# Attention and a long convolution on one core: a range guard with a second path, and three rewrites around the normalisation

## The chip, the cores and the metric

The kernel runs on one core of a Trainium2 chip. A core has five engines that run side by side, each with its own queue of instructions: PE (TensorE, the matrix unit; PEld in the profile is its weight load), DVE (VectorE), ACT (ScalarE), POOL (GpSimd) and SP (SyncE, which here only issues DMAs). They wait for one another through semaphores. The metric is device time of one execution in microseconds (us); less is better.

## The reference

Two independent results stand side by side in the output, columns 0 to 511 and 512 to 1023:

```python
# A: attention, S = 2048 tokens, D = 512, H = 32 heads of 16
qkv = (x @ wqkv) ...                                   # q, k, v of every head
scores = einsum("bhqd,bhkd->bhqk", q, k) * (Dh ** -0.5)
p = softmax(scores, axis=-1)
a = einsum("bhqk,bhkd->bhqd", p, v) ... @ wo
# B: a short and a long causal convolution with gates
kv = k_shift * v            # k_shift: 4 taps
y = long causal convolution of kv with ssm_k (per channel, length S) + kv * ssm_D
b = q * y
```

The inputs x and the weights have a standard deviation of 0.05, so q and k have 0.05 * 0.05 * sqrt(512) = 0.057, and a score is some thousandths. Every exponential is close to 1, and each row sum is close to 2048 times the constant factor with which the kernel scales its exponentials.

## The kernel before

**Attention.** The 32 heads are taken in 32 groups `n`; a group is four heads (one for each 32-row strip of the matrix unit) times 512 queries. Scores are made transposed, keys on partitions: one block is 128 keys by 512 queries of one head, so that a group has 16 x 4 = 64 blocks and the whole problem 2048. Four blocks of different heads can run beside each other on the four row strips (`qk_mm`, L838). A block's exponential is taken in one of two ways:

- on ACT, `exp` of two or three blocks (128x1024 or 128x1536) in one instruction from the PSUM banks into `PT` (`emit_exp`, L865);
- on DVE, one block per step at most: L901 reads the bank and makes a 16-bit fixed-point number in `PTD`, and for two blocks at a time three passes over SBUF (L929 mantissa, L934 square, L938 octave) make of it two float16 factors' terms, so that such a block goes into the next product as two matmuls of half weight.

The product with V (PV, `emit_pv`, L977) accumulates in bank `PVB`: four heads on four column strips run beside each other when four matmuls of four different heads stand next to each other. I call such a set of neighbours a pass. V has columns of ones behind its 16, so the row sum of the exponentials (the softmax's denominator) comes out of the same accumulation.

When a group is complete, `finish_group` does the following on DVE: transpose the bank to `DT` (L1084), reciprocal of the sums into `DR` (L1091), product with the reciprocals into `DTN` (L1095), and, after each second group, a transpose of `DTN` back to `OTN` (L1104), which is the weight operand of the output projection (L521 as unit "op", L1161 at the end). The last group is finished in four parts of 128 queries (`finish_last`, L1118, L1125, L1128, L1133).

**Convolution.** It is 512 channels of Toeplitz products (L1252) from rows `WR` that SP fetches from a scratch in memory, 512 KB at a time; results go through L1267 (DVE), L1279 (PE) and L1286 (DVE).

**Who decides the order.** No engine schedules itself: the program is written out once by a planner in the same file, step by step. Step `T` is one exponential of ACT; between two steps the planner puts PV passes, projections, convolution lags and, where PE would idle, filler matmuls of zero weights (L1502) that keep the matrix unit's clock up. It keeps a clock of its own for each engine, from constants at the head of the file (how many blocks to look ahead `LOOK`, how many blocks of a group must be left so that DVE may take one `GAP`, how close to the next exponential PE may still be given work `MARGIN`, and so on). `flow` holds the DVE work that can be moved; `urgent` work is put in when it is due; `locking` notes a time in which POOL is busy, and passes of kind "p" (L929, L934, L938) are not started in it. `feed_wr` and `on_op` pace the 512 KB loads against the fetching of PE's instructions.

**The end.** After the last exponential come the last PV passes, the last part of `finish_last`, the last projection, two copies (ACT L1584, DVE L1582), two output DMAs, and SP's wait for all output DMAs.

## Time and profile before

| | us |
|---|---|
| median of 3 runs (738.21 to 739.79) | 738.93 |
| the profiled execution | 737.82 |
| its span, first to last instruction | 736.0 |
| busy: ACT / DVE / PE / POOL | 722.2 / 705.1 / 698.3 / 98.9 |
| ACT's exponentials: 483 of 128x1024, 200 of 128x1536, 3 of 128x2048 | 719.9 busy, 3.0 idle before them |
| granted clock of the matrix unit | 0.998 of full speed |

How to read it: the profile's busy time of a group of instructions counts overlaps once, while "mean ns" is the length of one, with the part that overlaps its neighbours. "Idle before" is the time in which the engine had nothing in flight ahead of an instruction of the group, and the name behind the arrow is what ended that wait. The rows themselves stand in the prediction.

### The profile page before, as it was taken

To read this page: it belongs to the slowest core of one execution; us is meant where nothing else is said; L and a number is where in the kernel's file an instruction comes from. 1 tells how busy PE (TensorE), PEld (TensorE's weight loads), DVE (VectorE), ACT (ScalarE), POOL (GpSimd) and SP (SyncE) were. 2 spreads that over 40 slices of the span, in tenths; PEclk is the share of its full clock that TensorE was granted. 3 is DMA by queue.
4 is the path that set the end of the run, shared out by engine and by line. 5 is a ranking of instruction groups with operands and counts; after the bars stand their busy time and mean duration, and the time that the engine had idled before them with its cause. 6 is when DMAs were issued, how large, how long until landed. Compare 5 with 4: busy or idle time off the path is not lost.

```text
span 736.0 us, 32656 instructions
## 1 busy us (share of the span) xinstructions
PE 698.3 (95%) x14748; PEld 317.9 (43%) x14755; DVE 705.1 (96%) x1449; ACT 722.2 (98%) x690; POOL 98.9 (13%) x172
## 2 busy tenths in 40 slices
PE   8999999999999999999999999999999999999997
PEld 4333344445444444444444344444433443434455
DVE  3999999999999999999999999999999999989996
ACT  6999999999999999999999999999999999999997
POOL 7202102010023002001201300220021202010000
PEclk9999999999999999999999999999999999999999
DMA  9899655678797788677676777775857775585211
GB/s 181 227 253 307 173 194 189 218 235 251 264 258 263 245 285 244 229 229 260 181 225 217 228 261 231 229 264 167 294 188 261 238 263 179 201 273 193 103 45 32
DMA packets 73721, 161.50 MB, mean 219 GB/s; under 512 B 34064, under 2 KB 37776, under 8 KB 73200
## 3 DMA queue, kind: packets, MB, share of 16 engines
q1 hardware_dynamic: 66400, 150.43, 63.7%
q0 software_dynamic: 5984, 8.66, 4.0%
q8 instruction: 117, 1.92, 1.0%
q10 hardware_dynamic: 1200, 0.33, 0.2%
q14 instruction: 20, 0.16, 0.1%
HBM read 142.61 MB, written 6.42 MB: 202 GB/s over the span
## 4 chain that ended last, share of the span: by engine, by line
ACT 64%; DVE 24%; PE 10%; issue 0%
ACT PT L865 64%; DVE PTD L901 10%; DVE PTD L934 5%; PE PS L838 3%; DVE PTD L938 3%; DVE PTD L929 3%; PE PS L977 3%; PE PS L1252 2%; DVE KV L609 1%; DVE DT L1084 1%; PE PS L521 1%; PE PS L682 1%; DVE KTo L596 0%; DVE VA L625 0%; PE PS L1502 0%
## 5 line engine op out<-in xcount | busy, mean ns | idle before, releaser
L865 ACT ACTIVATE PT<-PS 128x1024 bf16<-128x1024 f32 (+2 forms) x686 | 719.9, 1261 | 3.0 <-PE PS L838 2.0
L901 DVE TENSOR_SCALAR PTD<-PS 128x512 uint16<-128x512 f32 x470 | 313.7, 680 | 7.8 <-PE PS L838 7.5
L838 PE MATMUL PS<-QT,KTo 32*128 32x512 bf16 (+2 forms) x2248 | 270.0, 365 | 20.3 <-ACT PT L865 9.5
L977 PE MATMUL PS<-PT,VA 128*32 128x512 bf16 (+2 forms) x1733 | 185.6, 369 | 1.9 <-DVE VA L625 1.3
L1252 PE MATMUL PS<-WR,KV 128*26 128x128 bf16 (+8 forms) x8192 | 186.7, 219 | 0.7 <-issue 0.5
L1252 PEld LDWEIGHTS PS<-WR,KV 128*32 128x32 bf16 (+7 forms) x8192 | 136.3, 94 | 56.6 <-issue 32.7
L934 DVE TENSOR_TENSOR PTD<-PTD 128x1024 f16<-128x1024 f16 x235 | 157.5, 678 | 0.1
L977 PE MATMUL PS<-PTD,VA 128*32 128x512 f16 (+1 forms) x1030 | 152.8, 363 | 0.5 <-DVE PTD L938 0.5
L838 PEld LDWEIGHTS PS<-QT,KTo 32*128 32x128 bf16 x2248 | 71.4, 91 | 180.5 <-ACT PT L865 121.6
L374 POOL DMA_DIRECT2D QT<-QS x120 | 61.0, 516 | 356.3 <-DVE QS L587 354.5
L938 DVE TENSOR_SCALAR PTD<-PTD 128x1024 uint16<-128x1024 uint16 x235 | 95.6, 411 | 0.2
L929 DVE TENSOR_SCALAR PTD<-PTD 128x1024 uint16<-128x1024 uint16 x235 | 93.5, 415 | 0.1
L977 PEld LDWEIGHTS PS<-PT,VA 128*32 128x32 bf16 x1733 | 46.6, 94 | 91.6 <-issue 74.2
L1502 PE MATMUL PS<-IDN,ZW 128*32 128x128 bf16 (+3 forms) x223 | 48.4, 298 | 0.0
L977 PEld LDWEIGHTS PS<-PTD,VA 128*32 128x32 bf16 x1030 | 40.9, 95 | 9.4 <-DVE PTD L938 1.4
L374 POOL DMA_DIRECT2D out_dram<-OUTA x15 | 8.9, 591 | 113.9 <-DVE OUTA L1169 113.9
L1502 PEld LDWEIGHTS PS<-IDN,ZW 128*32 128x32 bf16 x223 | 17.0, 96 | 14.8 <-issue 7.9
L1084 DVE STREAM_TRANSPOSE DT<-PS 128x512 f32<-128x512 f32 x31 | 21.9, 706 | 0.3 <-PE PS L977 0.2
L521 PE MATMUL PS<-xT,WKV 128*32 128x512 bf16 (+1 forms) x256 | 18.4, 376 | 3.7 <-DVE DT L1084 2.2
L575 PE MATMUL PS<-WKV,xT 128*128 128x128 bf16 x256 | 19.3, 220 | 1.5 <-DVE DT L1084 0.6
L521 PE MATMUL PS<-xT,WQ 128*32 128x512 bf16 x240 | 17.9, 384 | 2.4 <-DVE DT L1084 2.0
L575 PEld LDWEIGHTS PS<-WKV,xT 128*128 128x128 bf16 x256 | 14.4, 98 | 9.0 <-issue 3.8
(72 smaller groups left out, 243.1 us busy)
## 6 DMA issues: line engine op xcount, KB each, us to landing
WR<-kz_scratch SPq DMA_DIRECT2D x256, 512.0 KB, 5.3
KV<-KV SPq DMA_DIRECT2D x16, 256.0 KB, 6.6
kz_scratch<-WR SPq DMA_DIRECT2D x1, 2176.0 KB, 8.3
QN<-in_B_q_dram POOLq DMA_DIRECT2D x8, 256.0 KB, 5.2
out_dram<-QN POOLq DMA_DIRECT2D x8, 256.0 KB, 3.1
QT<-QS POOLq DMA_DIRECT2D x120, 16.0 KB, 4.3
out_dram<-OUTA POOLq DMA_DIRECT2D x15, 128.0 KB, 3.0
QN<-in_B_ssm_k_dram SPq DMA_DIRECT2D x1, 1024.0 KB, 7.7
```

What stands on the lines that cost most here:

```text
L374: f(outp, inp).then_inc(dsem.sem, 16)
L521: ins = e.matmul(dst[g:g + 32], lhsT=w[:, g:g + 32], rhs=rhs, tile_position=(0, g), **kw)
L575: ins = e.matmul(PS[:, bank, 128 * j:128 * j + 128], lhsT=xT[:, dc, (4 * sc + j) * 128:(4 * sc + j + 1) * 128], rhs=WV[:, dc, o * 128:(o + ...
L838: ins = e.matmul(PS[:, bank, i * w:i * w + w], lhsT=KTo[32 * s:32 * s + 32, OF[n_] % 2, kt * 128:(kt + 1) * 128], rhs=QT[32 * s:32 * s + 3 ...
L865: h = act.op(lambda e: e.activation(PT[:, p0:p0 + n, :], src, ACT.Exp, scale=EXP_SCALE, bias=EXP_BIAS), [h, free], us=(0.065 + 0.4257 * n, ...
L901: h_f = urgent(lambda e: e.tensor_scalar(fix_u, PS[:, bank, :], FIX_ADD, FIX_HI, ALU.add, ALU.min), [h, h_ptd.get(i - R_PTD)], slack=S_FX)
L929: st["h"] = dve.op(lambda e: e.tensor_scalar(mant_u, fix_u, MANT, HALF_BITS, ALU.bitwise_and, ALU.bitwise_or), [st["h"]], us=us)
L934: st["h"] = dve.op(lambda e: e.tensor_tensor(mant, fix, mant, ALU.mult), [st["h"]], us=us)
L938: h = dve.op(lambda e: e.tensor_scalar(fix_u, fix_u, OCTAVE, ONE_MORE, ALU.bitwise_and, ALU.bitwise_or), [st["h"]], us=us)
L977: ins = e.matmul(dst, lhsT=w, rhs=rhs, start=first, stop=last, tile_position=(0, 32 * s))
L1252: ins = e.matmul(PS[32 * g:32 * g + 2 * ((30 - d) // 2 + 1), BGB, 128 * kk:128 * kk + w], lhsT=kv, rhs=WR[:, (4 * qd + g) % R_W, S - 64 * ...
L1502: pe.op(lambda e, s=s, k=k, rhs=rhs, bank=bank, rows=rows, c0=c0, first=first: e.matmul(PS[32 * s:32 * s + rows, bank, c0:c0 + 128 * k], l ...
```

## The change

**The guard.** The kernel's two exponentials hold only while the row sums stay in a range. The changed kernel checks each reciprocal: `all_ok` puts four small instructions on POOL after every second group (and for each part of the last): clamp the reciprocals to the range, subtract, compare with zero, add to a count `OKS`. Behind everything else DVE sums the count (L1643), subtracts it from what it must be (L1644), PE adds that over the partitions (L1646), DVE turns it into an integer `BADI` (L1648), and each of the five engines loads that word into a register and branches: on zero to the end, otherwise into a second program that does the attention again with the exact maximum of each row. Ahead of the branch (2 planned operations on POOL and SP, 3 on ACT, 24 on DVE, 40 on PE) stands a prefetch hint for the branch. SP's wait for the output DMAs comes after the branch. With the given inputs the row sums are near 2048 * 2^-2 * 1.507 = 772, and the accepted range is 32 to 16384.

**Pair transposes.** q's columns are written in another order (`halves`, `in_pairs`), so that two heads' 16-bit values stand next to each other and the transpose back to `OTN` can move 32-bit pairs: 128x256 instead of 128x512 elements.

**Products with the reciprocals on POOL.** In `finish_group` L1095 moves from DVE to POOL (L1142), under `locking`; `DR` gets four buffers instead of two. In the last group they stay on DVE.

**PV gathered.** In `pv_step` a pass with fewer than four members is held back unless the ring of `PTD` buffers is full or the group must close; groups that must close wait up to three more steps for their DVE blocks.

Some planner constants change too.

```diff
-LOOK = 30
+DV_FREE = 0
+CLOSE_ALL = 1
+LOOK = 28
+HARD = 3
+LATE_BY = 0.2
-GAP = 20
+GAP = 18
-MARGIN = 0.15
+MARGIN = 0.1
-SLACK = 1.5
+SLACK = 2.0
+HOLD = 1.0
+HELD = 2
+MULT = (0.8, 0.95)
...
+    def halves(x):
+        return x.rearrange("p (a h i) -> p a h i", h=2, i=32)
+    def in_pairs(x):
+        return x.rearrange("p (a i h) -> p a h i", i=32, h=2)
...
-                if len(run) < 4 and not close and not old and len([x for x in bl if x[0] in on_dve]) < DV_MIN and T < end[0]:
+                if len(run) < 4 and not close and not old and T < end[0] and (len([x for x in bl if x[0] in on_dve]) < DV_MIN or ring_free() > DV_FREE):
+                    break
+                if CLOSE_ALL and len(run) < 4 and close and not late and not old and len(bl) < len([x for x in acts + dves if sub(x[0]) == (n, j)]) and n < NL:
                     break
...
+    def all_ok(n, r, h):
+        w = r.shape[1]
+        a, b, c = (OKS[:, i, 0:w] for i in range(3))
+        h_ok[n] = pool.op(lambda e: e.tensor_scalar(a, r, 1.0 / D_MOST, 1.0 / D_LEAST, ALU.max, ALU.min), [h, h_okn[0]], us=(0.1, 0.2))
+        h_ok[n] = pool.op(lambda e: e.tensor_tensor(b, a, r, ALU.subtract), [h_ok[n]], us=(0.1, 0.2))
+        h_ok[n] = pool.op(lambda e: e.tensor_scalar(a, b, 0.0, None, ALU.is_equal), [h_ok[n]], us=(0.1, 0.2))
+        h_ok[n - 1] = h_ok[n] = h_okn[0] = pool.op(lambda e: e.tensor_tensor(c, c, a, ALU.add), [h_ok[n], h_okn[0]], us=(0.1, 0.2))
...
         def mult(us):
             r = n % 2
-            h_mul[n] = dve.op(lambda e: e.tensor_tensor(
...
+            h_mul[n] = locking(pool.op(lambda e: e.tensor_tensor(
+                heads_of(dtn, r), halves(dt)[:, :, :, 0:DH], over(DR[:, n % 4, :], 8), ALU.mult), [st["h"], h_otn.get(p - 2)], us=MULT), MULT[0] - 0.2)
...
-            h_otn[(p, i1)] = h_otn[p] = dve.op(lambda e: e.transpose(out=OTN[:, p, sl], in_=dtn[:, sl]), deps, us=us)
+            h_otn[(p, i1)] = h_otn[p] = dve.op(lambda e: e.transpose(out=OTN[:, p, sl].bitcast(PAIR), in_=dtn[:, sl].bitcast(PAIR)), deps, us=us)
...
-    for ds in d_outA + d_outB + [d_outE]:
-        sp.op(lambda e, ds=ds: e.wait_ge(ds.sem, ds.n), inc=False)
+    h_bad = dve.op(lambda e: e.tensor_reduce(OKS[:, 0, 0:1], OKS[:, 2, :], mybir.AxisListType.X, ALU.add), [h_okn[0]])
+    h_bad = dve.op(lambda e: e.tensor_scalar(BAD[:, :], OKS[:, 0, 0:1], -1.0, float(NQB * NG * 16), ALU.mult, ALU.add), [h_bad])
+    h_bad = pe.op(lambda e: e.matmul(PS[0:1, bank, 0:1], lhsT=BAD[:, :], rhs=VA[:, 0, 0, DH:DH + 1], start=True, stop=True),
+                  [h_bad, bank_free[bank]], kind="F")
+    h_bad = dve.op(lambda e: e.tensor_copy(BADI[:, :], PS[0:1, bank, 0:1]), [h_bad])
...
+    def decide(e, eng, geng, ahead):
+        eng.run(e, ahead)
+        e.wait_ge(*h_bad)
+        r = e.alloc_register("bad")
+        e.reg_load(r, BADI[0:1, 0:1])
+        names = [f"{e.engine.name}_{x}" for x in ("again", "over")]
+        e.br_eq(r, 0, names[1], names[0]).branch_hint(eng.hint)
+        with nc.body(names[0], valid_engines=[e.engine]):
+            geng.run(e)
+            e.br(names[1])
+        nc.switch_bb(names[1])
```

What the planner makes of it is shown by the order of the two built programs, at three places.

First, DVE and POOL at the end of a group. In the rows, `DT` is the transposed bank, `DR` the reciprocals, `DTN` the product, `PTD` the fixed-point blocks. DVE before, at the end of an odd group:

```order
L1084 STREAM_TRANSPOSE DT<-PS 128x512
L938 TENSOR_SCALAR PTD<-PTD 128x2x512
L1091 RECIPROCAL DR<-DT 128x16
L938 TENSOR_SCALAR PTD<-PTD 128x2x512
L609 TENSOR_TENSOR KV<-PS,OUTA 128x4x16x4 x2
L1095 TENSOR_TENSOR DTN<-DT,DR 128x16x16
L929 TENSOR_SCALAR PTD<-PTD 128x2x512
L1104 STREAM_TRANSPOSE OTN<-DTN 128x512
```

DVE now, at the end of an odd group:

```order
L1130 STREAM_TRANSPOSE DT<-PS 128x512
L956 TENSOR_SCALAR PTD<-PTD 128x2x512
L1137 RECIPROCAL DR<-DT 128x16
L961 TENSOR_TENSOR PTD<-PTD 128x2x512
L928 TENSOR_SCALAR PTD<-PS 128x512
L1155 STREAM_TRANSPOSE OTN<-DTN 128x256
```

and POOL now, over the same kind of place (`OKS` is the guard's scratch and count; QT and QN are the DMAs that POOL issues):

```order
L389 DMA QT<-QS 16x512 x8
L1142 TENSOR_TENSOR DTN<-DT,DR 128x8x2x16
L1120 TENSOR_SCALAR OKS<-DR 128x32
L1121 TENSOR_TENSOR OKS<-OKS,DR 128x32
L1122 TENSOR_SCALAR OKS<-OKS 128x32
L1123 TENSOR_TENSOR OKS<-OKS 128x32
L389 DMA QN<-in_B_q_dram 128x4x256 x4
L1142 TENSOR_TENSOR DTN<-DT,DR 128x8x2x16 x2
```

The product has left DVE's queue for POOL's, where the four guard instructions follow it; the transpose back on DVE now waits for POOL and has half the elements.

Second, PE around the end of a group (`QT,KTo` are scores, `PT,VA` and `PTD,VA` PV, `WR,KV` the convolution). Before:

```order
L838 MATMUL PS<-QT,KTo 128x512 x3
L977 MATMUL PS<-PT,VA 32x512 x13
L977 MATMUL PS<-PTD,VA 32x512 x3
L838 MATMUL PS<-QT,KTo 128x512 x3
L977 MATMUL PS<-PT,VA 32x512 x2
L977 MATMUL PS<-PTD,VA 32x512 x2
L1252 MATMUL PS<-WR,KV 20x128 x4
```

Now:

```order
L865 MATMUL PS<-QT,KTo 128x512 x3
L1004 MATMUL PS<-PT,VA 32x512 x7
L1004 MATMUL PS<-PTD,VA 32x512
L1004 MATMUL PS<-PT,VA 32x512 x3
L1004 MATMUL PS<-PTD,VA 32x512
L865 MATMUL PS<-QT,KTo 128x512 x3
L1004 MATMUL PS<-PT,VA 32x512 x2
L1004 MATMUL PS<-PTD,VA 32x512 x2
L1309 MATMUL PS<-WR,KV 12x128 x4
```

PV still comes in bursts of twelve and sixteen between two sets of scores; members of `PT` and `PTD` are now mixed so that a pass is full.

Third, DVE at the very end. Before:

```order
L1125 RECIPROCAL DR<-DT 128x4
L1128 TENSOR_TENSOR DTN<-DT,DR 128x4x16
L1133 STREAM_TRANSPOSE OTN<-DTN 128x128
L1169 CAST OUTA<-PS 128x512
L1582 CAST QT<-PS 128x256
L1589 UNCONDITIONAL_BRANCH
```

Now:

```order
L1184 STREAM_TRANSPOSE OTN<-DTN 128x64
L1639 CAST QT<-PS 128x256
L1643 TENSOR_REDUCE OKS<-OKS 128x1
L1644 TENSOR_SCALAR BAD<-OKS 128x1
L1648 CAST BADI<-PS 1x1
L1769 TENSOR_LOAD BADI
L1771 COMPARE_AND_BRANCH
```

Behind the last copy stand three more instructions with one of PE between them, and the branch on the loaded word.

Counted over the whole main path, from the two orders:

| | before | now |
|---|---|---|
| ACT exponentials 128x1024 / 128x1536 / 128x2048 | 483 / 200 / 3 | 485 / 198 / 3 |
| blocks on DVE (L901, now L928) | 470 | 472 |
| products with reciprocals on DVE / on POOL | 35 / 0 | 4 / 31 |
| guard instructions on POOL | 0 | 80 and one memset |
| copies of the convolution L1267 (now L1324): 512 / 384 / 256 / 128 wide | 6 / 6 / 7 / 8 | 5 / 6 / 6 / 14 |
| PV matmuls of 512 columns, and the passes they make | 2431 in 671 | 2434 in 631 |
| steps of a two-block exponential with 11 or more PV matmuls of 512 columns | 28 | 36 |
| filler matmuls (L1502, now L1559) | 223 | 255 |

## The prediction

> **What bounds the kernel now.** I read the page's busy shares first, then the groups of ACT and DVE with shapes kept apart, then the waits of ACT, then the timeline at the places where ACT had waited, and last the end of the program.

> ```profile
> span 736.0 us, 32656 instructions
> PE 698.3 (95%) x14748; PEld 317.9 (43%) x14755; DVE 705.1 (96%) x1449; ACT 722.2 (98%) x690; POOL 98.9 (13%) x172
> ACT 64%; DVE 24%; PE 10%; issue 0%
> ```

> ACT is busy 98% of the span and carries most of the chain that ended last. DVE and PE stand at 96% and 95%, but PE is topped up by fillers and DVE by blocks that the planner hands over. POOL is nearly free.

> ```profile
> L865 ACT ACTIVATE PT<-PS 128x1024 bf16<-128x1024 f32 x483 | 472.8, 1132 | 2.1 <-PE PS L838 1.3
> L865 ACT ACTIVATE PT<-PS 128x1536 bf16<-128x1536 f32 x200 | 295.1, 1562 | 0.4 <-PE PS L838 0.3
> L865 ACT ACTIVATE PT<-PS 128x2048 bf16<-128x2048 f32 x3 | 5.7, 1889 | 0.5 <-PE PS L838 0.5
> ```

> Only 3.0 us of idle time stand before 686 exponentials, so the kernel is one stream of ACT work with a head and a tail. Its rate comes from an undisturbed stretch:

> ```profile
> 599.08 41.91 ACT L865 ACTIVATE PT<-PS 128x1536 bf16<-128x1536 f32 x40
> L865 ACT ACTIVATE PT<-PS 128x1024 bf16<-128x1024 f32 x28 | 27.0, 1166 | 0.0
> L865 ACT ACTIVATE PT<-PS 128x1536 bf16<-128x1536 f32 x12 | 17.5, 1566 | 0.0
> 8.04 12.31 ACT L865 ACTIVATE PT<-PS 128x2048 bf16<-128x2048 f32 x10 [0.50 <-PE PS L838]
> 713.97 16.51 ACT L865 ACTIVATE PT<-PS 128x1024 bf16<-128x1024 f32 x17
> ```

> A third block in an instruction costs 1562 - 1132 = 430 ns. The 40 instructions (28 of two blocks, 12 of three) took 41.91 us; less 12 x 0.43, and less the 0.2 us by which the last one outlasts its turn, that is 0.914 us for a step of two blocks. The whole stream at that rate is 686 x 0.914 + 200 x 0.43 + 3 x 0.76 (1889 - 1132) + 0.2 = 715.5 us. It ran from 8.04 to 713.97 + 16.51 = 730.48, which is 722.4 us. So 6.9 us were lost in it, 3.0 of them as visible idle time and the rest as starts a little late, hidden in the overlap. The change can gain by fewer blocks on ACT, by less of these 6.9 us, or in the tail.

> **Where ACT lost time.** The largest loss in the stream is this one:

> ```profile
> 72.76 0.75 DVE L929 TENSOR_SCALAR PTD<-PTD 128x1024 uint16<-128x1024 uint16 x2
> 73.43 0.68 DVE L934 TENSOR_TENSOR PTD<-PTD 128x1024 f16<-128x1024 f16 x1
> 74.03 2.00 DVE L901 TENSOR_SCALAR PTD<-PS 128x512 uint16<-128x512 f32 x3
> 74.77 0.53 PE L838 MATMUL PS<-QT,KTo 32*128 32x512 bf16 x3 [0.94 <-DVE PTD L901]
> 75.34 1.02 ACT L865 ACTIVATE PT<-PS 128x1024 bf16<-128x1024 f32 x1 [0.66 <-PE PS L838]
> 76.64 19.37 ACT L865 ACTIVATE PT<-PS 128x1536 bf16<-128x1536 f32 x18 [0.27 <-PE PS L838]
> ```

> DVE ran passes without a gap, so the L901 that frees a bank came late, PE waited 0.94 us for it, and ACT stood still for 0.66 + 0.27 = 0.93 us. The other kind is smaller and more frequent, a burst of PV between two sets of scores:

> ```profile
> 422.46 4.19 ACT L865 ACTIVATE PT<-PS 128x1024 bf16<-128x1024 f32 x4
> 423.29 1.04 PE L977 MATMUL PS<-PT,VA 128*32 128x512 bf16 x13
> 424.27 0.10 PEld L838 LDWEIGHTS PS<-QT,KTo 32*128 32x128 bf16 x3 [0.42 <-issue]
> ```

> Sixteen PV matmuls (13, and 3 from PTD) held PE from 423.29 to 424.27; the four exponentials took 4.19 us where 4 x 0.914 + 0.2 = 3.86 were due, a loss of 0.33 us.

> **The change, part by part.** The profiled execution took 737.82 us with its span of 736.0, 1.11 us under the median of 738.93; I make the sum as a difference and add it to the median.

> *Blocks on ACT.* The order shows two blocks moved to DVE: 200 to 198 instructions of three blocks, 483 to 485 of two. With 686 steps as before that is 2 x 0.43 = -0.86 us on the path.

> *Products, transposes and blocks on DVE.*

> ```profile
> L901 DVE TENSOR_SCALAR PTD<-PS 128x512 uint16<-128x512 f32 x470 | 313.7, 680 | 7.8 <-PE PS L838 7.5
> L934 DVE TENSOR_TENSOR PTD<-PTD 128x1024 f16<-128x1024 f16 x235 | 157.5, 678 | 0.1
> L938 DVE TENSOR_SCALAR PTD<-PTD 128x1024 uint16<-128x1024 uint16 x235 | 95.6, 411 | 0.2
> L929 DVE TENSOR_SCALAR PTD<-PTD 128x1024 uint16<-128x1024 uint16 x235 | 93.5, 415 | 0.1
> L1095 DVE TENSOR_TENSOR DTN<-DT,DR 128x256 bf16<-128x256 f32 x31 | 12.8, 412 | 0.0
> L1104 DVE STREAM_TRANSPOSE OTN<-DTN 128x512 bf16<-128x512 bf16 x15 | 10.5, 701 | 0.0
> L1133 DVE STREAM_TRANSPOSE OTN<-DTN 128x128 bf16<-128x128 bf16 x4 | 1.2, 309 | 0.1
> L1267 DVE CAST YB<-PS 128x128 bf16<-128x128 f32 x8 | 2.3, 282 | 0.4 <-PE PS L977 0.2
> ```

> The 31 products leave: -12.8 us. A transpose costs (701 - 309) / 384 = 1.02 ns a column, so 256 pairs take 0.44 us (if pairs cost what single elements do; bounds 0.31, as if width were nothing, and 0.70, as if nothing were saved): 15 x -0.26 = -3.9. Two blocks come: 2 x (680 + (678 + 411 + 415) / 2) = +2.9. Four more copies of the convolution, mostly narrow: about +0.6. DVE falls by 13 us to some 692. None of it is on the path by itself, since ACT is; what it buys is that a late L901 gets rarer. I take the 0.93 us loss at 75 us as gone (bounds: 0, as that stretch's passes are still there, and -2, all of ACT's visible waits for L838). The re-laid evacuations of q (L587, L708) keep their price: only their access pattern changes, and L1267, which reads its columns in reverse, takes 282 ns for 128 of them, in line with 680 for 512 at about 1.04 ns a column.

> *PV gathered.* 671 passes become 631. At 0.98 us for the four passes above, 40 x 0.24 = 10 us of PE; 32 more fillers fill part of it, so PE's share stays. What ACT feels is the bursts: steps with 11 or more PV matmuls behind a two-block exponential rise from 28 to 36. Upper bound: 0.33 us each, but 28 of these would be 9.2, more than all that was lost; leaving out 0.5 at the start and 0.93 at 75 us, their mean is at most (6.9 - 1.4) / 28 = 0.20. Lower bound 0. I take a third of the upper one, because most of the lost time lies in small pieces elsewhere: 8 x 0.065 = +0.5 (0 to +1.6). The smaller MARGIN works in the same direction and is in this term.

> *Work added to POOL.*

> ```profile
> L666 POOL TENSOR_SCALAR_AFFINE_SELECT OTN<-SHK 128x2048 bf16<-128x2048 bf16 x1 | 2.0, 2013 | 4.5 <-DMA SHK<-in_B_shift_k_dram 4.5
> L470 POOL MEMSET PAT<- 1x64 bf16 x2 | 0.3, 141 | 0.1
> L374 POOL DMA_DIRECT2D QT<-QS x120 | 61.0, 516 | 356.3 <-DVE QS L587 354.5
> 388.93 1.57 POOL L374 DMA_DIRECT2D out_dram<-QN  x2 [28.91 <-PE PS L838]
> 390.07 1.00 DVE L929 TENSOR_SCALAR PTD<-PTD 128x1024 uint16<-128x1024 uint16 x2
> ```

> No two-input operation ran on POOL. A product of 256 columns lies between 2.0 x 256 / 2048 = 0.25 us and the whole 2.0 us; I take 0.8, between them and nearer the lower end, whose work per column is the nearer. 31 x 0.8 + 80 x 0.14 = 36 us in 637 idle ones. Behind a product in POOL's queue stand QT and output DMAs; eight QT issues take 4.1 us and are planned about 20 steps ahead, so nobody waits for a microsecond there. The transpose back and the next group's first transpose wait for the product, and groups are 23 us apart. Cost 0, if DVE and POOL don't meet. When they do, the row at 390 shows it: two L929 took 1.00 us instead of 0.75 while POOL issued DMAs. That 0.25 us cost ACT nothing there.

> [...]

> *The tail.*

> ```profile
> 733.24 0.42 DVE L1582 CAST QT<-PS 128x256 bf16<-128x256 f32 x1 [0.56 <-PE PS L1161]
> 733.69 0.36 SPq L374 DMA_DIRECT2D out_dram<-QT  x1
> out_dram<-QT SPq DMA_DIRECT2D x1, 64.0 KB, 1.8
> L1091 DVE RECIPROCAL DR<-DT 128x16 f32<-128x16 f32 x31 | 7.4, 237 | 0.0
> L694 DVE TENSOR_SCALAR MASK<-PS 128x2 f32<-128x2 f32 x1 | 0.2, 159 | 4.2 <-PE PS L690 4.2
> L690 PE MATMUL PS<-PAT 1*128 1x1 bf16 x2 | 0.2, 170 | 0.0
> L482 ACT ACT_TABLE_LOAD x1 | 1.3, 1283 | 1.8 <-issue 1.8
> ```

> The last transpose loses 64 columns: -0.06 us. DVE is done at 733.66, the output lands at 733.69 + 1.8 = 735.5. Beside that landing the guard runs: sum 0.24 (like the reciprocal), 0.16, PE 0.17, 0.16, and four handovers of about 0.06: ready at 734.6. Loading the register and branching lies between 0.1 and ACT's table load of 1.3 us: done between 734.7 and 735.9, that is 0 to 0.4 us behind the landing. I take +0.2. If the cover is gone (the branch target must be fetched), the second rival prices it.

> Sum: -0.86 - 0.93 + 0.5 + 0 - 0.06 + 0.2 = -1.15 us. 738.93 - 1.15 = 737.8. That is within 0.2% (1.5 us), about what a measurement of this kernel can tell from no change.

> **The rivals.**

> 1. *POOL and DVE block each other* (slower). Place: L1142 against L956, L961 and L965. Price: once as at 75 us, 0.93 us of ACT. Without my gain of 0.93 the sum is -0.2; five such meetings in 31 products give +4.4, 743.4, and two are enough to pass +1.5. For it: the passes fill 347 of DVE's 705 us and the planned place of a product is only as good as the plan. Against: the planner keeps passes out of its windows, DVE has 13 us to catch up with, and 120 QT issues of 0.5 us beside the passes did little. As a case, three meetings: 741.5.

> 2. *The branch is not covered.* Each engine fetches its end only after the compare. Price: the nearest fetch is the 64 KB landing of 1.8 us, so the end comes at about 735.9 + 1.8 instead of 735.9: +1.8, 739.6. Against: the hints stand microseconds ahead. [...]

> 3. *The relief reaches ACT in full.* DVE is 13 us and PE 10 us lighter, the pacing of loads is stricter, and half of the 6.9 us goes: -0.86 - 3.45 + 0.14 = -4.2, 734.8. For it: the largest loss, at 75 us, was late DVE work. Against: more bursts, less margin.

> 4. *The change does not do what it says for ACT*: PV in bursts keeps the losses, DVE's freed time turns into waiting for POOL's windows: -0.86 + 0.5 + 0.14 = -0.2, 738.7.

> That the second path itself runs, 1024 exponentials of 0.914 us, would add over 900 us; sums near 772 are far inside the range, and I give it no chance worth a number.

> **How the numbers follow.** Forecast 0.34 (a third of it beyond -1.5 us); relief in full 0.25, all faster; no effect 0.09, all same; branch not covered 0.08, half of it same, half slower by what else is lost; blocking 0.24, slower. Faster 0.11 + 0.25 = 0.36; same 0.23 + 0.09 + 0.04 = 0.36; slower 0.04 + 0.24 = 0.28. The forecast's own range, from its terms' bounds, is 736.3 to 739.5. With the third rival's middle below and the first rival's three meetings above, 734.5 to 741.7 leaves out about 2 in 10.

> **What would show it.** Right: 485 and 198 exponentials, last one ending near 728.6 in a span near 734.9; DVE busy near 692; no DVE wait for POOL; SP's last wait still for the output. Wrong: ACT's idle time above 3 us with L838 behind L928 or behind passes longer than 0.42 us beside L1142; or more than 5.6 us between ACT's last exponential and the end.

## The result: slower by 0.8%

The changed kernel took 744.44 us (median of 6 runs, 742.72 to 745.18), the kernel before 737.92 beside it (6 runs). The ratio is 1.0082, 95% interval [1.0065, 1.0099]: slower, and outside the range forecast (734.5 to 741.7). The profiled execution took 745.18 us with a span of 743.4, so the span grew by 7.4 us over the 736.0 of before. A few executions of these kernels ran far above the rest of their kind, as the profiled one of e9 below (750.08 us); the ratios leave them out, and the profile of e9 is not used.

The head of the page of the changed kernel and its chain by engine:

```profile
span 743.4 us, 32868 instructions
PE 699.2 (94%) x14787; PEld 316.2 (43%) x14787; DVE 697.0 (94%) x1430; ACT 721.7 (97%) x690; POOL 150.5 (20%) x284
...
ACT 78%; PE 12%; DVE 7%; issue 1%; DMA 1%
```

Its groups of ACT, shapes kept apart:

```profile
L892 ACT ACTIVATE PT<-PS 128x1024 bf16<-128x1024 f32 x485 | 472.9, 1117 | 5.2 <-PE PS L865 4.3 <-PE PS L1004 0.2
L892 ACT ACTIVATE PT<-PS 128x1536 bf16<-128x1536 f32 x198 | 290.7, 1545 | 2.9 <-PE PS L865 2.8
L892 ACT ACTIVATE PT<-PS 128x2048 bf16<-128x2048 f32 x3 | 5.7, 1889 | 0.5 <-PE PS L865 0.5
```

ACT has the blocks that were forecast (485 and 198), but its idle time before them rose from 3.0 to 8.6 us. I cut the span into three pieces, each from the trace:

| us | before | after | difference |
|---|---|---|---|
| start to the first exponential | 8.04 | 7.80 | -0.24 |
| first exponential to the end of the last (the stream) | 722.43 | 727.58 | +5.15 |
| end of the last exponential to the end of the span | 5.57 | 8.04 | +2.47 |

Within the stream I call *lost* what the exponentials end later, one behind the other, than the usual 0.915 us for two blocks, 1.342 us for three and 1.77 us for four. Summed over the trace that is 6.7 us before and 12.7 after: +6.0 lost, and -0.9 of work.

**Where the stream lost it.** The waits of the changed kernel (total, times, longest, in us); "issue" means that nothing which the profile shows held the engine up:

```profile
PEld PS L1004 <- issue: 79.6, 337, 1.5
...
PEld PS L1309 <- issue: 28.1, 118, 1.2
...
PEld PS L865 <- issue: 17.3, 42, 2.5
...
ACT PT L892 <- PE PS L865: 7.6, 13, 2.1
...
PEld PS L865 <- DVE PTD L928: 4.2, 9, 0.5
```

and the same of before:

```profile
PEld PS L977 <- issue: 74.5, 328, 0.4
...
PEld PS L1252 <- issue: 32.7, 142, 0.8
...
PEld PS L838 <- issue: 19.0, 53, 0.7
...
ACT PT L865 <- PE PS L838: 2.0, 5, 0.7
```

The sums are alike; the longest are not. Before, PE never stood longer than 0.8 us for "issue"; after, up to 2.5. The worst of these in the timeline of after, with the last row load that SP issued ahead of it:

```profile
520.50 0.61 SPq L389 DMA_DIRECT2D WR<-kz_scratch  x1
...
525.63 0.10 PEld L865 LDWEIGHTS PS<-QT,KTo 32*128 32x128 bf16 x3 [2.48 <-issue]
525.63 0.39 PE L865 MATMUL PS<-QT,KTo 32*128 32x512 bf16 x3 [2.29 <-issue]
...
526.07 1.45 ACT L892 ACTIVATE PT<-PS 128x1536 bf16<-128x1536 f32 x1 [2.08 <-PE PS L865]
```

PE waited for no bank and no tile, ACT stood still, and PE issued nothing for 2.48 us. What it waited for shows in another queue of the page:

```profile
q8 instruction: 118, 1.93, 1.0%
```

The queue moved 118 packets, 1.93 MB, 16 KB each. PE has 30067 records in the trace, which is 117.4 times 256, so I take q8 for PE's own code and a packet for a block of 256 instructions; PE enters a new block every 5.6 us (median).

I call a wait of more than 0.44 us for "issue" ahead of a weight load, later than 20 us, a *stop*: 4 before (2.7 us together), 10 after (10.0 us). They are of two kinds. Eight of the ten after (8.7 us) stand at one and the same place of PE's code, record 193 or 194 of each 256, so a block begins there; each of them ends 2.3 to 2.6 us after a packet of q8 began, the one above after the packet that began at 523.36. Before has two such stops, of 0.76 and 0.62 us. I call these *stops at an entry*. The other two of after (529.4 and 530.8) stand elsewhere in the code, behind the longest stop, where the matrix unit's granted clock was 0.50 (527.4 to 530.8); the other two of before (76.0 and 77.4) stand behind the late DVE pass, where it was 0.50 too (74.9 to 78.3).

The packet that a stop waits for is late because it starts late. Taking as the entry into a block the instruction ten ahead of the one on which the stops stand, since some packets start before that one, the mean delay from the entry to the start of a packet is 1.7 us before and 2.0 after, over 4 us at 2 entries before and at 8 after. The delay goes with the row loads in flight at the entry, that is, issued by SP and not yet landed. In the trace of after the mean delay is 1.1 us with none in flight (26 entries), 1.2 with one (18), 2.1 with two (49), 3.2 with three (16) and 3.7 with four (7); one entry met six. A row load takes 5.4 us to land; ahead of the late packet at 523.36 SP had issued six of 512 KB between 514.7 and 520.5, and three were still in flight when it began.

**Where the end lost it.** The waits of SP's queue after:

```profile
SPq L1777 <- PEq L1777: 3.1, 1, 3.1
...
SPq L1769 <- DVE BADI L1648: 0.3, 1, 0.3
```

and the last rows of ACT, SP and DVE in the timeline:

```profile
737.43 0.38 ACT L1641 ACTIVATE QT<-PS 128x256 bf16<-128x256 f32 x1 [2.06 <-PE PS L1212]
...
737.89 0.36 SPq L389 DMA_DIRECT2D out_dram<-QT  x1
...
738.40 0.15 DVE L1648 CAST BADI<-PS 1x1 int32<-1x1 f32 x1 [0.26 <-PE PS L1646]
```

L1777 is the barrier behind the branch. The records of the sequencers give the rest: every engine loads its register at 738.58 (0.62 to 0.65 us) and branches at 739.2 to 739.3; SP sees all outputs landed at 740.0; PE, DVE and SP are at the end block between 739.7 and 740.2, ACT only at 743.05. So the guard was ready beside the landing, as forecast, and then ACT alone was 3 us late.

### The profile page after: what moved, and what is told of

Its sections match the earlier page's. It is cut to its first block, busy times and chain, and to the rows that moved or that the text cites. A ratio compares the mean times of both kernels' runs of the same rounds, so it can differ in the third digit from the quotient of the medians.

```text
span 743.4 us, 32868 instructions
## 1 busy us (share of the span) xinstructions
PE 699.2 (94%) x14787; PEld 316.2 (43%) x14787; DVE 697.0 (94%) x1430; ACT 721.7 (97%) x690; POOL 150.5 (20%) x284
## 3 DMA queue, kind: packets, MB, share of 16 engines
q1 hardware_dynamic: 66400, 150.43, 64.1%
q8 instruction: 118, 1.93, 1.0%
## 4 chain that ended last, share of the span: by engine, by line
ACT 78%; PE 12%; DVE 7%; issue 1%; DMA 1%
ACT PT L892 78%; PE PS L865 4%; PE PS L1004 3%; DVE PTD L928 3%; PE PS L1309 3%; DVE PTD L961 1%; DVE PTD L965 1%; DVE PTD L956 1%; DMA xT<-in_A_x_dram 1%; PE PS L536 1%; DVE KV L636 0%; PE PS L1559 0%; DVE WR L681 0%; PE PS L1212 0%; DVE DT L1130 0%
## 5 line engine op out<-in xcount | busy, mean ns | idle before, releaser
L928 DVE TENSOR_SCALAR PTD<-PS 128x512 uint16<-128x512 f32 x472 | 314.6, 680 | 15.7 <-PE PS L865 14.8
L865 PE MATMUL PS<-QT,KTo 32*128 32x512 bf16 (+2 forms) x2248 | 269.2, 365 | 20.3 <-ACT PT L892 7.1
L1004 PE MATMUL PS<-PT,VA 128*32 128x512 bf16 (+2 forms) x1734 | 189.0, 368 | 4.8 <-issue 2.8
L1309 PE MATMUL PS<-WR,KV 128*28 128x128 bf16 (+8 forms) x8192 | 177.9, 219 | 1.7 <-issue 1.6
L961 DVE TENSOR_TENSOR PTD<-PTD 128x1024 f16<-128x1024 f16 x236 | 158.9, 680 | 0.2
L1309 PEld LDWEIGHTS PS<-WR,KV 128*30 128x30 bf16 (+7 forms) x8192 | 135.1, 94 | 52.4 <-issue 28.1
L1004 PE MATMUL PS<-PTD,VA 128*32 128x512 f16 (+1 forms) x1028 | 148.7, 367 | 0.1
L865 PEld LDWEIGHTS PS<-QT,KTo 32*128 32x128 bf16 x2248 | 71.2, 91 | 182.5 <-ACT PT L892 125.3
L965 DVE TENSOR_SCALAR PTD<-PTD 128x1024 uint16<-128x1024 uint16 x236 | 97.8, 417 | 0.2
L956 DVE TENSOR_SCALAR PTD<-PTD 128x1024 uint16<-128x1024 uint16 x236 | 93.5, 416 | 0.0
L1142 POOL TENSOR_TENSOR DTN<-DT,DR 128x256 bf16<-128x256 f32 x31 | 23.5, 757 | 297.6 <-DVE DR L1137 297.5
L1559 PE MATMUL PS<-IDN,ZW 128*32 128x512 bf16 (+3 forms) x255 | 58.4, 309 | 0.0
L1004 PEld LDWEIGHTS PS<-PTD,VA 128*32 128x32 bf16 x1028 | 39.2, 95 | 6.8 <-issue 1.2
L1559 PEld LDWEIGHTS PS<-IDN,ZW 128*32 128x32 bf16 x255 | 19.7, 96 | 17.8 <-issue 9.7
L536 PE MATMUL PS<-xT,WQ 128*32 128x512 bf16 x240 | 17.5, 383 | 0.9 <-DVE DT L1130 0.5
```

The costliest lines, as they stand in the source:

```text
L536: ins = e.matmul(dst[g:g + 32], lhsT=w[:, g:g + 32], rhs=rhs, tile_position=(0, g), **kw)
L865: ins = e.matmul(PS[:, bank, i * w:i * w + w], lhsT=KTo[32 * s:32 * s + 32, OF[n_] % 2, kt * 128:(kt + 1) * 128], rhs=QT[32 * s:32 * s + 3 ...
L928: h_f = urgent(lambda e: e.tensor_scalar(fix_u, PS[:, bank, :], FIX_ADD, FIX_HI, ALU.add, ALU.min), [h, h_ptd.get(i - R_PTD)], slack=S_FX)
L956: st["h"] = dve.op(lambda e: e.tensor_scalar(mant_u, fix_u, MANT, HALF_BITS, ALU.bitwise_and, ALU.bitwise_or), [st["h"]], us=us)
L961: st["h"] = dve.op(lambda e: e.tensor_tensor(mant, fix, mant, ALU.mult), [st["h"]], us=us)
L965: h = dve.op(lambda e: e.tensor_scalar(fix_u, fix_u, OCTAVE, ONE_MORE, ALU.bitwise_and, ALU.bitwise_or), [st["h"]], us=us)
```

## The experiments

A summary first; "ratio" is to the kernel before, run beside it on the same chip (its median there was 736.5 to 738.4 us); stream, end, lost and stops (in brackets those at an entry) are of the one profiled execution, defined as above. A profiled execution lies up to 3 us off the median of its kernel, so small differences between profiles mean little.

| run | us | ratio, 95% interval | stream | end | lost | stops (at an entry) |
|---|---|---|---|---|---|---|
| before (first profile) | 737.92 | | 722.4 | 5.6 | 6.7 | 4 (2) |
| after | 744.44 | 1.0082 [1.0065, 1.0099] | 727.6 | 8.0 | 12.7 | 10 (8) |
| e1 quarter rows | 737.05 | 0.9984 [0.9958, 1.0009] | 721.6 | 8.6 | 6.7 | 1 (1) |
| e2 hint 16 | 744.56 | 1.0107 [1.0069, 1.0145] | 727.8 | 8.0 | 12.9 | 7 (7) |
| e3 SLACK 1.5 | 742.89 | 1.0075 [1.0052, 1.0097] | 724.8 | 8.8 | 8.6 | 3 (2) |
| e4 products on DVE | 744.54 | 1.0128 [1.0064, 1.0192] | 726.0 | 9.9 | 10.3 | 5 (4) |
| e5 hint 150 | 740.72 | 1.0027 [0.9999, 1.0056] | 726.4 | 5.1 | 11.5 | 7 (4) |
| e6 no end | 741.89 | 1.0043 [1.0011, 1.0074] | 729.0 | 5.0 | 14.1 | 11 (8) |
| e7 before, SLACK 2.0 | 741.87 | 1.0030 [0.9996, 1.0065] | 728.8 | 5.0 | 12.2 | 4 (2) |
| e8 before, quarter rows | 736.80 | 0.9976 [0.9954, 0.9999] | 720.5 | 5.6 | 4.7 | 0 (0) |
| e9 SLACK 1.5, hint 150 | 741.21 | 1.0031 [1.0012, 1.0050] | | | | |
| e10 SLACK 1.0, hint 150 | 741.78 | 1.0039 [1.0020, 1.0059] | 727.3 | 7.2 | 11.4 | 7 (7) |
| e11 old pacing, hint 150 | 741.76 | 1.0061 [1.0017, 1.0105] | 723.2 | 7.2 | 10.0 | 4 (4) |
| e12 MARGIN 0.15, hint 150 | 739.27 | 1.0030 [0.9996, 1.0064] | 722.0 | 5.8 | 5.8 | 2 (2) |
| e13 before, SLACK 1.4 | 737.87 | 0.9991 [0.9969, 1.0014] | 724.2 | 5.9 | 7.6 | 5 (3) |
| e14 before, KV_DUE 15 | 742.52 | 1.0061 [1.0038, 1.0085] | 726.6 | 6.3 | 9.2 | 2 (2) |
| e15 before, Q_DUE 20 | 741.27 | 1.0043 [1.0013, 1.0073] | 726.1 | 5.0 | 8.6 | 2 (2) |
| e16 loads behind the entry | 746.32 | 1.0096 [1.0068, 1.0123] | 726.4 | 11.8 | 11.5 | 8 (7) |
| e17 rows in halves | 799.05 | 1.0868 [1.0797, 1.0938] | 785.9 | 5.2 | 71.1 | 32 (28) |
| e18 e12 with halves | 797.40 | 1.0833 [1.0803, 1.0864] | 779.5 | 5.8 | 63.3 | 23 (18) |

### Does PE's code come late because of the row loads?

```diff
+            w = S if k < R_W else S // 4
-            src = bass.AP(tensor=kz_ap.tensor, offset=kz_ap[row, 0].offset, ap=[[1, 64], [64 * LKZ, 2], [1, S]])
-            h_wr[qd] = dma(sp, d_wr[qd % 3], WR[:, k % R_W, :], src, ...)
+            src = bass.AP(tensor=kz_ap.tensor, offset=kz_ap[row, 0].offset, ap=[[1, 64], [64 * LKZ, 2], [1, w]])
+            h_wr[qd] = dma(sp, d_wr[qd % 3], WR[:, k % R_W, 0:w], src, ...)
```

> The kernel after the change with the loads of the WR ring cut: from the second use of a slot on, only a quarter of each row (128 KB of 512 KB) is loaded, so three quarters of those loads are left out and the convolution's later columns are computed from stale rows; plan and order of all engines stay. Theory A (PE's next instructions come late because row loads of 512 KB stand in the same DMA queues; the profile after has eight stops of PE put down to issue, 0.5 to 2.5 us, and ACT loses some 6 us by them): PE's stops over 0.44 us fall from eight to two or fewer, ACT's stream from its first to its last exponential falls from 727.6 us to about 722, time near 739 us. Rival B (the plan itself, its bursts of PV, or POOL and DVE in each other's way, costs the time): the stream stays within 1 us of 727.6 and the time near 744 us. The end of the program stays the same by both.

Measured: 737.05 us, 7.4 less than after, with the stream at 721.6 (727.6 after) and one stop left of ten. The profiled executions differ by 5.8 us. The waits of this run, and the loads' queue on its page:

```profile
PEld PS L1004 <- issue: 74.7, 328, 0.4
...
PEld PS L1310 <- issue: 25.4, 112, 0.2
...
PEld PS L865 <- issue: 14.2, 39, 0.8
```

```profile
q1 hardware_dynamic: 66400, 54.09, 29.8%
```

No matmul, exponential or pass was changed or moved; only bytes left queue q1 (150.43 MB and 64.1% after, 54.09 MB and 29.8% here). PE's long waits for "issue" went with them, and 6.0 us of the stream. The mean delay of a code packet fell from 2.0 to 1.1 us. Theory A holds: the loss of the stream is PE's code coming late while rows are loaded. The end part stayed (8.6), as expected.

The control is the same cut in the kernel before (the same diff).

> The kernel before the change with the loads of the WR ring cut in the same way as in the first run (three quarters of those loads left out from the second use of a slot on). Theory A: before loses little by late code (two stops, 0.76 and 0.62 us, besides those behind the late DVE pass at 75 us), so its stream goes from 722.4 to 721 or 721.5 and the time down by 1 to 1.4 us, near 736.7; the cut takes 6 us from after and 1 from before. Rival (lighter loads speed any such kernel up): 5 to 7 us down, 731 to 733.

Measured: 736.80, 1.1 us less than before, stream 720.5, no stop. So the cut is not a general speed-up: it takes 7.4 us from after and 1.1 from before, and with it the two streams differ by 1.1 us instead of 5.2.

### Is it POOL and DVE?

```diff
-            h_mul[n] = locking(pool.op(lambda e: e.tensor_tensor(
-                heads_of(dtn, r), halves(dt)[:, :, :, 0:DH], over(DR[:, n % 4, :], 8), ALU.mult), [st["h"], h_otn.get(p - 2)], us=MULT), MULT[0] - 0.2)
+            h_mul[n] = dve.op(lambda e: e.tensor_tensor(
+                heads_of(dtn, r), halves(dt)[:, :, :, 0:DH], over(DR[:, n % 4, :], 8), ALU.mult), [st["h"], h_otn.get(p - 2)], us=us)
```

> The kernel after the change with its 31 products by the reciprocals back on DVE. Theory A (the loss is PE's late code): DVE busy goes from 697 to some 709 us, the stops of PE remain six to ten, time within 2 us of 744.4. Rival (products on POOL block DVE's passes, or the wait for POOL's windows costs ACT): the lost 5 us come back, time near 739 us.

Measured: 744.54, 5 stops, longest 2.2 us. The time did not move, and the rival's 739 is far off; my first rival falls. In the profile two changes cancel: the stream is 1.6 us shorter and the end 1.9 us longer, because the last output landed 2.1 us later behind the last exponential. As the edit makes a new plan, the 1.6 us cannot be laid to the products. At the end DVE, too, reached the end block late here (742.8), which became the key to the next question.

### Why is ACT late at the end?

```diff
-            decide(e, act, gact, 3)
+            decide(e, act, gact, 16)
```

> The kernel after the change with ACT's hint for the branch placed 16 operations before its end instead of 3. Theory (in the profile after, ACT's last code block begins at 731.35 us, before its hint, so the branch's target is fetched only after the branch, and ACT's last DRAIN comes 3.3 us after the other engines are at the end block): from ACT's last exponential to the end of the span 8.0 us becomes 5 to 5.5, time down by 2.5 to 3 us, near 741.7. Rival (ACT's branch is slow whatever the hint): 744.4, no change.

Measured: 744.56, end part 8.0, ACT's last DRAIN at 742.80, three microseconds behind the others. A miss: a hint 19 us ahead of the branch (it ran at 719.7, the branch at 739.1) did nothing. So lead in time alone is not what counts. The places of the code packets led to another theory, and the next run tried it:

```diff
-            decide(e, act, gact, 3)
+            decide(e, act, gact, 150)
```

> The kernel after the change with ACT's hint for the branch 150 operations before its end instead of 3. Sixteen did nothing. In the traces ACT's code packets come at its instruction 49, 178, 306, 431 and 559, 128 apart, and none follows before its branch at 697; DVE's packet behind its hint (1453) comes at 1473, just where it enters its last block, while in the run with the products on DVE, where DVE's hint (1475) stands behind that point, DVE too ended late. Theory: the target takes the place of the block that would be fetched as the block of the branch is entered, so the hint must stand before that point, for ACT before instruction 559; then ACT's last DRAIN falls from 3.3 us behind the other engines to about 0, the part from the last exponential to the end of the span from 8.0 to 5 to 5.5 us, time near 741.7. Rival (ACT ends late by whatever hint): 744.4.

Measured: 740.72, end part 5.1, ACT's DRAIN at 738.45 and so before PE's and DVE's (738.55 and 738.62). The wait of SP at the barrier, 3.1 us after, is now:

```profile
SPq L1769 <- DVE BADI L1648: 0.3, 1, 0.3
SPq L1777 <- PEq L1777: 0.2, 1, 0.2
```

So the 3 us are ACT's late branch, and a hint that stands early enough takes them away. How early is known only within bounds. ACT's hint at its instruction 692 or 678 left ACT late (after and e2; also e1, e3 and e4), at 544 to 546 it did not (e5, and the later runs with hint 150); the branch is instruction 697. By the expectation's reading of the second queue of this kind (`q14 instruction: 25, 0.20, 0.1%` on the page of after), which is an inference from the packets' times, ACT's last packet ahead of the branch comes at instruction 559, between the two. DVE fits the same order: a hint at 1453 with a packet at 1473 behind it was in time, one at 1475 behind the packet at 1454 (e4) was not. That the hint must precede the entry into the branch's own block is not shown: ACT's packets come 128 instructions apart, so the next entry would lie near 687, and e2's hint stood ahead of that and did nothing. From its packet at instruction 49 (53.9 us in after) to the one at 559 (594.1) ACT ran 128 instructions in some 136 us, so by this reading its hint has to stand far earlier than DVE's.

What the guard costs in all is the question of the next run: the sum of the flags, the register loads, the branches and the second program are left out.

```diff
-    h_bad = dve.op(lambda e: e.tensor_reduce(OKS[:, 0, 0:1], OKS[:, 2, :], mybir.AxisListType.X, ALU.add), [h_okn[0]])
...
     def decide(e, eng, geng, ahead):
         eng.run(e, ahead)
-        e.wait_ge(*h_bad)
...
```

> The kernel after the change without its guard's end: the sum of the flags, the register loads, the branches and the second path are left out; the comparisons on POOL stay. Theory: the stream of exponentials stays as after (stops of PE too), and the part from the last exponential to the end goes from 8.0 us back to 5.3 to 5.8 us, time near 741.9. Rival (the tail's 2.5 us come from elsewhere, for example from the last PV and transposes): no change in the tail, 744.4.

Measured: 741.89, end part 5.0, the stream as long as after's or longer (729.0, 11 stops). With the hint in the right place the end with the guard (5.1) is as short as the end without it (5.0): the guard hides behind the last output, as the forecast had it, once ACT's branch does.

### What in the change brings the late code?

The loads' pacing was the suspect: SLACK, how far a row load may be planned to end past the entry into a block, went from 1.5 to 2.0 us.

```diff
-SLACK = 2.0
+SLACK = 1.5
```

> The kernel after the change with the planner's SLACK put back from 2.0 to 1.5 us, so that a load's planned end may lie 0.5 us less past the crossing into the next block of PE's code. Theory A (loads planned to end later past a crossing delay the fetch of PE's code): the mean delay from a crossing to the fetch falls from 2.0 us towards 1.5, PE's stops over 0.44 us from eight to about four, time down by 2 to 5 us, 739.5 to 742.5. Rival B (SLACK doesn't carry the loss): within 1 us of 744.4, stops as many as before.

> The kernel before the change with SLACK at 2.0 us instead of 1.5 and nothing else. Theory A1 (SLACK alone makes the fetches of PE's code late): PE's stops over 0.44 us rise from about four to six or more, time up by 2 to 5 us, 740 to 743. Rival A2 (the loss belongs to the new plan's loads as a whole, not to SLACK alone): within 1 us of 737.9.

Measured: after with 1.5 took 742.89 (ratio 1.0075, against 1.0082 for after, no difference by the intervals), though its profile had only 3 stops. Before with 2.0 took 741.87, 4.0 above the median beside it, which looked like support; but its ratio, 1.0030 [0.9996, 1.0065], shows no clear difference, and of its 12.2 us lost, 3.4 stand at one place at 723.75, without a stop of PE. The next runs put SLACK together with the early hint:

```diff
-            decide(e, act, gact, 3)
+            decide(e, act, gact, 150)
-SLACK = 2.0
+SLACK = 1.5
```

> The kernel after the change with SLACK 1.5 us and ACT's hint 150 operations before its end. If the two losses add up as they were measured apart (SLACK alone: 742.9; hint alone: 740.7 against 744.4 to 744.6), the time is 739 to 739.5 us: stream near 724.8, end part 5.1. Rival (the stream of 724.8 in the earlier run was luck of one profile): 740.7 as with the hint alone.

> The kernel after the change with SLACK 1.0 us and ACT's hint 150 operations before its end. Theory A (loads that are planned to end past a crossing make the fetch late): fewer stops of PE than with 1.5, stream 722 to 724 us, time 736.5 to 738.5, at or under before's 737.9. Rival (with tighter pacing the row loads come late for the convolution, or its matmuls bunch): stream over 725, time over 740.

> The kernel after the change with the pacing rules of before: SLACK 1.5 us, no holding back (HELD so large that it never acts) and no LONGEST, with ACT's hint 150 operations before its end; NEED_C stays 18. Theory A (SLACK carries the loss, HELD and LONGEST don't): as with SLACK 1.5 alone, 738.5 to 740. Rival (the new holding rule costs or saves the time): over 1.5 us apart from the run with SLACK 1.5 and the same hint.

Measured: 741.21, 741.78 and 741.76, all three a little over the 740.72 of the hint alone, with intervals that overlap its own. Tighter pacing gained nothing that shows; the stops moved to other places (e10: 2.6 us at 717.2, 1.1 at 708.0). Taking SLACK, HELD and LONGEST back does not bring the time back. As each of these edits also makes a new plan, that is not a proof that they cost nothing.

```diff
-MARGIN = 0.1
+MARGIN = 0.15
-            decide(e, act, gact, 3)
+            decide(e, act, gact, 150)
```

> The kernel after the change with MARGIN back from 0.1 to 0.15 us (its value before the change) and ACT's hint 150 operations before its end; SLACK stays 2.0. Theory A (SLACK carries the loss; MARGIN only shifts the plan): stops of PE as many as with the hint alone, stream 725 to 728, time 739.5 to 742. Rival (the smaller MARGIN, which lets PV bursts closer to the scores, carries the loss): stream near 723, time near 737.5.

Measured: 739.27, with runs from 737.05 to 745.91. Its profile (stream 722.0, 2 stops, 5.8 us lost) has the shortest stream of all the changed kernels with full loads, but it is of the fastest of its runs, and by the intervals (1.0030 [0.9996, 1.0064] and 1.0027 [0.9999, 1.0056]) it cannot be told from the hint alone. Not decided.

That left the thought that any new plan loses, because the plan of before is a good one among its neighbours. Three edits of the kernel before test it; two of them change no rule of the loads:

```diff
-SLACK = 1.5
+SLACK = 1.4
```

> The kernel before the change with SLACK 1.4 us instead of 1.5. Theory A1 (the size of SLACK carries the loss): as before or a little under, 737 to 738. Theory A2 (PE's code comes late wherever a row load happens to be in flight as a block of code is entered; the plan of before is one that meets this seldom, and any new plan loses some microseconds whatever the sign of the edit): 739 to 742, with stops of PE of 0.5 to 2.5 us at new places.

```diff
-KV_DUE = 16
+KV_DUE = 15
```

> The kernel before the change with KV_DUE 15 instead of 16: a due time that has nothing to do with the loads' pacing, so the plan is new and nothing else. Theory A2 (any new plan loses): 739 to 742. Rival A1 (only the loads' pacing rules cost): within 1 us of 737.9.

```diff
-Q_DUE = 21
+Q_DUE = 20
```

> The kernel before the change with Q_DUE 20 instead of 21, a second new plan without any change of pacing. Theory A2: 739 to 742. Rival A1: within 1 us of 737.9.

Measured: 737.87 (no change), 742.52 (+4.2 to the 738.36 beside it) and 741.27 (+2.9). Two due times that are not meant for the loads cost as much as the whole change with ACT's hint put right (740.72, 2.8 over the median beside it). But the way is only partly the one that I expected. The end of the stream in e14:

```profile
719.26 0.75 DVE L938 TENSOR_SCALAR PTD<-PTD 128x1024 uint16<-128x1024 uint16 x2
719.73 0.78 PEld L977 LDWEIGHTS PS<-PTD,VA 128*32 128x32 bf16 x24 [2.32 <-DVE PTD L938]
719.74 1.04 PE L977 MATMUL PS<-PTD,VA 128*32 128x128 f16 x24 [2.15 <-DVE PTD L938]
...
721.92 1.45 ACT L865 ACTIVATE PT<-PS 128x1536 bf16<-128x1536 f32 x1 [2.76 <-PE PS L977]
```

Here a closing set of PV matmuls waits for DVE's last passes and ACT stands 2.76 us; e15 has 2.34 at the same place. Both plans also gave ACT 204 instructions of three blocks instead of 200, which is 4 x 0.43 = 1.7 us of work. Late code is two stops in each. So a new plan of this kernel cost between nothing and 4 us in these three, by whichever collision it fell into; in after's case it is late code.

### Can the loads be kept out of the way?

```diff
-GATE = 2
+GATE = 3
-SLACK = 2.0
+SLACK = -1.0
-            decide(e, act, gact, 3)
+            decide(e, act, gact, 150)
```

> The kernel after the change with ACT's hint 150 operations before its end, and row loads almost only just behind the entry into a block of PE's code: SLACK -1.0 us instead of 2.0, and up to three loads at once (GATE 3 instead of 2). Theory A (a load in flight at the entry delays the fetch): if fewer loads are in flight at entries, the mean delay of the fetch falls from 1.8 to 2.0 us towards 1.1 (as with the quarter rows), few stops of PE remain, stream 722 to 724, time 736 to 738.5. Rival (three loads in a row reach the next entry after all, or the convolution waits for its rows): stream 726 or more, time over 740.

Measured: 746.32, mean delay of the code packet 2.1 us, 8 stops: the rival. Three loads in a row do reach the next entry: three or more were in flight at 48 of 117 entries, against 24 in after and 20 in e5. And this plan left projections and their evacuations (L1212, L1220) behind the last exponential, an end part of 11.8 us.

```diff
-            src = bass.AP(..., offset=kz_ap[row, 0].offset, ap=[[1, 64], [64 * LKZ, 2], [1, S]])
-            h_wr[qd] = dma(sp, d_wr[qd % 3], WR[:, k % R_W, :], src, ...)
+            one, two = [bass.AP(..., offset=kz_ap[row, 32 * c].offset, ap=[[1, 32], [64 * LKZ, 2], [1, S]]) for c in range(2)]
+            h_wr[qd] = dma(sp, d_wr[qd % 3], WR[0:64, k % R_W, :], one, ..., more=[(WR[64:128, k % R_W, :], two)])
```

> The kernel after the change with ACT's hint 150 operations before its end and each row load of 512 KB issued as two of 256 KB on SP, one behind the other; plan and order of PE, ACT, DVE and POOL stay as in the run with the hint alone (740.7, stream 726.4). Theory C (PE's fetch waits for the load that is being worked off, so smaller loads let it through earlier): mean delay of the fetch from 1.8 us to about 1, stops of PE fewer, stream 722 to 724, time 737 to 738.5. Rival D (the fetch waits for all bytes in flight, in whatever pieces): delay and stops as before, time 740 to 741.5.

> The kernel of the run with MARGIN 0.15 and the early hint (739.3, stream 722.0 in its profile) with each row load issued as two of 256 KB: a try at a version under both kernels. Theory C: stops of PE fewer, 736 to 738. Rival D: 739 to 740, since its plan and its bytes stay.

Measured: 799.05 and 797.40; both theories missed. From the page of e17, the queue of the loads, the chain by engine and the loads; then its waits:

```profile
q1 hardware_dynamic: 70496, 150.45, 80.1%
...
ACT 42%; PE 37%; DVE 11%; issue 6%; DMA 3%; SPq 1%
...
WR<-kz_scratch SPq DMA_DIRECT2D x512, 256.0 KB, 5.7
```

```profile
PEld PS L1008 <- issue: 100.0, 354, 3.4
ACT PT L896 <- PE PS L869: 58.8, 58, 4.3
...
PEld PS L1314 <- issue: 52.1, 137, 3.2
```

After's loads for comparison:

```profile
WR<-kz_scratch SPq DMA_DIRECT2D x256, 512.0 KB, 5.4
```

A load of half the bytes into half the partitions, two of them issued one behind the other, took 5.7 us to land where the whole took 5.4. The same bytes held the DMA engines for 80.1% of a span of 798.5 us, which is 640 us, where e5 with whole rows had 63.4% of 739.3, which is 469. The halves were no lighter loads but twice as many long ones. Whether a truly smaller load would let the code through sooner stays open. As a dose, though, it lies on one line with e1 and after: 29.8%, 64.1% and 80.1% of DMA time in q1, 1, 8 and 28 stops at an entry, 6.7, 12.7 and 71.1 us lost (in e17 a part of them because rows themselves came late: "DMA" has 3% of the chain). The share alone does not decide: before has 63.7% and two stops at an entry, so it also matters where the loads fall.

No version that loads whole rows was faster than before. The two best are after with ACT's hint 150 operations ahead and the same with MARGIN 0.15: with the guard in them, neither can be told from before by its interval (1.0027 [0.9999, 1.0056] and 1.0030 [0.9996, 1.0064]).

## Why the prediction was wrong

The sum was 737.8 us, 1.15 under before, and the measured time went the other way: two terms failed, the tail and one that the sum did not have. The bounds of its terms add up to 736.0 to 740.0, a little wider than the 736.3 to 739.5 given; 744.44 lies outside both.

- **Blocks on ACT, -0.86: right.** 485 and 198 instructions; the stream's work fell by 0.9 us.
- **Late DVE at 75 us, -0.93: right in size, its reason not shown.** In the windows view of after the stretch where before had DVE's late pass has ACT busy for all of its 10 us (columns as in the first row), 9.07 in before:

```profile
core 0: us, PE busy (x) PEld busy (x) DVE busy (x) ACT busy (x) POOL busy (x), PEclk, DMA share, GB/s
70.00:80.00 10.00, 9.63 (x91) 2.71 (x90) 10.00 (x23) 10.00 (x11) 1.62 (x2) 1.00 0.81 235
```

  The products' leaving DVE is not what it takes: e4, with the products back on DVE, has ACT busy for 10.00 us there, too. The four new plans of before (e7, e13 to e15) have it busy for 9.13 to 9.48 us, so the gain comes with the change, but by something else in it.
- **DVE: half right.** I forecast a DVE busy near 692 and it is 697.0. The products went (-12.8) and the transposes cost 437 ns where 0.44 us was estimated, but the block passes grew by 4.5 us in sum, more than the two blocks' 2.9, which explains a part of the gap. It didn't matter.
- **More PV bursts, +0.5: not seen.** With light loads the changed kernel lost 6.7 us in its stream (3.0 of it in the first 39 us) and before 4.7; behind the first 39 us that is 3.6 against 4.4. Nothing is left for bursts.
- **POOL's work, 0: right.** A product took 757 ns (0.8 estimated), and e4 with the products on DVE took the same time. DVE's passes beside them kept their length (416, 680 and 417 ns, against 415, 678 and 411), DVE waited 0.7 us in all for POOL's products (L1155), and in the waits DVE's late L928 holds PE up 0.5 us at most. This was the rival to which I gave 0.24.
- **The tail, +0.2: the step that failed first.** The guard itself came as I timed it, and e5 and e6 show its cost with a proper hint to be about 0.1 us. But I took the branch as covered, because the hints "stand microseconds ahead". Microseconds were the wrong measure: ACT's hint ran 5.8 us and 5 instructions before its branch (19 us in e2), by the reading above behind ACT's last code packet, and ACT reached the end block only 3.75 us after its branch. The end grew by 2.5 us (8.04 against 5.57), and e5 took 3.7 us off the time. That was my second rival, at 0.08 and a price of +1.8. Its price was about right, but by luck, as it was the landing of a 64 KB output; it had every engine fetch its end late, while PE, DVE and SP were at the end block 0.06 to 0.9 us after their branches. Its chance was far too low: the program showed leads from 2 to 40 operations, and what ACT's and DVE's hints did went with the places of the code packets as I read them, not with the leads.
- **The term that was missing, +6.0: the larger failure.** I read PE's waits for "issue" in before (two of 0.76 and 0.62 us, apart from those behind the late DVE pass) as part of 6.9 us that could only shrink, and took the pacing constants as "stricter" without a price, in the third rival alone. The sum should have had a term "PE's code behind row loads", bounded by what before shows and by a row load's 5.4 us per meeting, for the plan is new and 256 loads meet 118 entries anew. The stops at an entry were 1.4 us in before's stream of 722 and 8.7 us in after's of 728.
- **What I can't name.** Which of the rewrites shifted the plan into these meetings is not settled; every rewrite moves the whole plan. Taking back SLACK, HELD and LONGEST or the products on POOL did not bring the time back, MARGIN is undecided, and the gathered PV and the pair transposes were not undone one by one.

## What to carry to other kernels

A kernel whose order is planned to the microsecond has a scatter of its own: before forecasting a change that replans it, ask what an idle edit of the planner costs (here 0 to +4.2 us for three edits), and take that into the range on the slow side. Look for waits put down to "issue" on the engine with the most instructions and ask what is loaded beside its code: here PE's long "issue" waits, up to 2.5 us, were no noise. In these runs ACT's and DVE's hints helped only where they ran ahead of what I read as the engine's last code packet before the branch (ACT's at instruction 544 to 546, not at 678; DVE's at 1453, not at 1475): count instructions, not time, and for an engine of few long instructions try the hint far earlier.

## What the runs showed of the hardware

```profile
515.00:523.00 8.00, 7.38 (x214) 3.61 (x204) 8.00 (x18) 8.00 (x9) 0.00 (x0) 1.00 0.78 250
523.00:533.00 10.00, 7.71 (x152) 2.76 (x144) 7.10 (x14) 7.15 (x8) 0.00 (x0) 0.83 0.66 227
533.00:540.00 7.00, 6.46 (x156) 2.93 (x149) 6.96 (x16) 7.00 (x8) 2.64 (x6) 1.00 0.76 238
```

  0.83 in the 10 us around it, 1.00 on both sides. Sets of scores at 528.06 and 529.36 took 0.61 us instead of 0.39, so this late packet cost more than its own wait. No run leaves the fillers out, so that they keep the clock up is the planner's purpose and not shown.
- A load of 256 KB into 64 partitions, issued in pairs, took as long to land as one of 512 KB into 128 (5.7 and 5.4 us), and the same bytes held the DMA engines for 640 us instead of 469.
- Loading one word into a register took 0.62 to 0.65 us on every engine, the compare and branch 0.07 to 0.08 us, on PE 0.40.
